# Retention and two feed-forward layers on one core: the lead-in in another order, with the first splits on VectorE

## The chip, the cores and the metric

The kernel runs on one core of a Trainium2 chip. The metric is the device time of one execution in microseconds (us); a kernel's figure is the median of several runs. A profile is one execution recorded by the hardware profiler; its span is a little shorter than the run's time. The engines are TensorE (PE; its weight loads are listed as PEld), VectorE (DVE), ScalarE (ACT), GpSimd (POOL) and SyncE (SP), which here issues all transfers.

## The reference

Retention with a decay per head (2 batches, 8 heads, 768 positions, head size 64), then two feed-forward layers on the 1536 x 512 result, all in float32:

```python
for t in range(S):
    state = gamma[None, :, None, None] * state + np.einsum('bhd,bhe->bhde', k[:, :, t], v[:, :, t])
    y[:, :, t] = scale * np.einsum('bhd,bhde->bhe', q[:, :, t], state)
...
x = np.ascontiguousarray(attn_out.transpose(0, 2, 1, 3)).reshape(B * S, H * D)
h = x @ w_in                                        # layer 1: 512 x 2048
g = np.maximum(h, 0.0) + np.log1p(np.exp(-np.abs(h)))
x = g @ w_out                                       # 2048 x 512
h = x @ w_in                                        # layer 2, other weights
g = h * (1.0 / (1.0 + np.exp(-h)))
out = g @ w_out
```

## The kernel before

**Retention in chunks.** A chunk is 128 positions of one batch. There are 12, numbered n = 0 to 11, and an even n and the next are the same positions of the two batches. For each chunk the kernel computes the scores (`att_scores`, L169, PE), multiplies them by the decay mask while it takes them out of PSUM (`att_mask`, L177, DVE), multiplies by V (`att_within`, L187), adds what the state of earlier chunks gives (`att_across`, L201, with `past`, the state copied by ACT at L159, and with queries scaled on GpSimd, `att_scale_q`, L128), and adds its own keys and values to the state (`att_state`, L149, with keys scaled on GpSimd, `att_scale_k`, L136). Chunks 0 and 1 have no across part. In names, `sc` are scores in PSUM, `scm` masked scores, `qp` and `kp` the scaled queries and keys, `py` a chunk's result in PSUM.

**Products in three parts.** The feed-forward products are made from a high and a low part of each operand: low times high, high times low, high times high. `att_split` makes the parts of a chunk's result: xhi is a rounded copy by ACT (L219), xlo the rest. With `spare=True` (chunks 0 and 1), ACT makes a second, unrounded copy (L222) and GpSimd subtracts (L223); otherwise DVE subtracts straight from PSUM (L225). Four chunks, all in one pair of tiles, are a block of 512 tokens.

**Weights** come as 64-bit floats, in units of 512 KB (128 x 512 values); unit u of the plan is converted by `w_exponent` (ACT, z, L272), then `convert`: `w_digits` (DVE, two operations, L279 and L280), `w_values` (DVE, four operations, L289 to L297, the last gives the low part wlo) and `w_split` (ACT, whi, L308, from the result `a` of L292). Three buffers hold raw units.

**The feed-forward steps.** `gemm1(i, half)` is 12 matmuls for half a tile h of hidden values: for i = 0 the halves are token columns 0 to 255 (chunks 0, 1) and 256 to 511 (chunks 2, 3), for others halves of the contraction. `act1` (ACT, L352 and L353) applies the function twice, rounded and not; `act2` (DVE, L359) subtracts. In the lead-in all h tiles share one bank of PSUM, so h1 can be written once `act1(0)` has read h0. `first(i)` is both halves and `act1`; `second(i)` is the second product.

**What sets the order.** The program is written in a fixed order, and each engine takes its instructions in the order in which the code emits them. All transfers are issued by SP in the order of the calls `att_load`, `qs_load`, `w_load` and of the single ones for `mask` and `cs`. `att_load(n, lo, hi)` loads parts lo to hi of chunk n: 0 and 1 are Q and K transposed (512 KB for the pair), 2 is V (256 KB), 3 is K (256 KB). The mask has 512 KB, `qs` 256 KB, `cs` 24 KB. The lead-in is L458 to L545; from L547 on, the later chunks alternate with feed-forward steps, and from L578 on there are feed-forward steps alone.

Of the kernel before, what the change touches and what calls it, by code (L numbers as in the profile page):

```python
# [75 lines left out]
def retention_ffn2_kernel(  # L76
# [133 lines left out]
    def att_split(n, spare=False):  # L210
        py = py_t.pop(n)
        blk, o = n // CPB, (n % CPB) * P
        if o == 0:
            x_t[0, blk] = (
                xpool.tile([P, NPAIR, BLK], F32R, tag="xhi", name=f"xhi{blk}"),
                xpool.tile([P, NPAIR, BLK], F32R, tag="xlo", name=f"xlo{blk}"),
            )
        hi, lo = (t[:, :, o : o + P] for t in x_t[0, blk])
        nc.scalar.activation(out=hi, in_=py, func=AF.Copy)  # L219
        if spare:  # L220
            full = epool.tile([P, NPAIR, P], F32, tag="t", name=f"y{n}")
            nc.scalar.activation(out=full, in_=py, func=AF.Copy)  # L222
            nc.gpsimd.tensor_tensor(out=lo, in0=full, in1=hi.bitcast(F32), op=ALU.subtract)  # L223
        else:
            nc.vector.tensor_tensor(out=lo, in0=py, in1=hi.bitcast(F32), op=ALU.subtract)  # L225
# [201 lines left out]
    def first(i):  # L427
        gemm1(i, 0)
        gemm1(i, 1)
        act1(i)  # L430
# [26 lines left out]
    with tc.manual_schedule():  # L457
# [5 lines left out]
        w_load(0)  # L463
        att_load(2, 0, 2)
        nc.sync.dma_start(out=cs, in_=cs_d)
        att_load(0, 3, 4)
        att_load(1, 3, 4)
        qs_load(1)
        att_load(3, 0, 2)
# [3 lines left out]
        att_load(4, 0, 2)  # L473
        att_load(2, 3, 4)
        att_load(3, 3, 4)
        nc.scalar.preload_act_table_set("softplus")
# [10 lines left out]
        att_split(0, spare=True)  # L487
        w_exponent(0)
        att_within(1)
        att_split(1, spare=True)  # L490
        convert(0)
        att_scores(2)
# [6 lines left out]
        qs_load(2)  # L499
        att_load(4, 2, 3)  # L500
        att_load(5, 2, 3)
        w_load(2)
        att_load(4, 3, 4)
        att_load(5, 3, 4)
        att_mask(2)
        att_scale_q(2)
        att_scale_q(3)
        att_scores(3)
        att_mask(3)
        att_within(2)  # L510
        att_across(2)
        w_exponent(1)
        w_digits(1)
        att_split(2)
        att_within(3)
        att_across(3)
        att_split(3)
        gemm1(0, 0)
        att_scale_k(2)
        att_scale_k(3)  # L520
        att_state(2)
        att_state(3)
        att_past()
# [4 lines left out]
        w_values(1)  # L528
        w_split(1)
        att_scale_q(4)  # L530
        att_scale_q(5)
        att_scores(4)
        att_scores(5)
        att_mask(4)
        att_mask(5)
        gemm1(0, 1)
        act1(0)
# [3 lines left out]
        att_scale_k(5)  # L541
        w_exponent(2)
        first(1)
        convert(2)
        act2(0)  # L545
# [98 lines left out]
```

## Time and profile before

| | before |
|---|---|
| time, median of 3 runs | 584.91 us (584.90 to 585.33) |
| profiled execution: time | 584.48 us |
| profiled execution: span | 582.3 us |
| PE busy in the span | 571.3 us (98%) |
| DVE, ACT, POOL busy | 372.4, 198.9, 46.4 us |
| the chain that ended last, by engine | PE 96%, DMA 1%, POOL 1% |
| first matmul of `first(1)` | 33.38 us |

The chain of work that ended last is followed back from the last instruction, at each step to what released it. Work that isn't on it costs nothing by itself. The granted clock (PEclk) is a share of 2.4 GHz.

### The profile page before, as it was taken

The numbers are of one execution on the slowest core, as the hardware profiler recorded it, in microseconds if no ns is written. First come the engines' busy times: TensorE is split into PE (matmuls) and PEld (weight loads), VectorE is DVE, ScalarE is ACT, GpSimd is POOL, SyncE is SP. The second block draws the span as 40 slices with busy tenths as digits, with TensorE's granted clock in tenths as the row PEclk, the third lists the DMA queues.
The fourth block names the chain that finished last, engine by engine and source line by source line (L and its number), as shares of the span: only waits on it lengthen the run. The fifth ranks groups of instructions, "written<-read, shape, count | busy, mean of one in ns | idle before, by whom it ended". The sixth has DMA issues, their size and how long they took to land.

```text
span 582.3 us, 7525 instructions
## 1 busy us (share of the span) xinstructions
PE 571.3 (98%) x3026; PEld 472.8 (81%) x3026; DVE 372.4 (64%) x611; ACT 198.9 (34%) x365; POOL 46.4 (8%) x38
## 2 busy tenths in 40 slices
PE   7899999999999999999999999999999999999997
PEld 4788888888888888888888888888888888888885
DVE  4889565755864866685769954575656854783332
ACT  2234153432432432342445542452333332342120
POOL 1816100000000000000213210000000000000000
PEclk9799999999999999999999999999999999999999
DMA  8987212311321222123113212122113212110111
GB/s 298 354 307 257 71 38 72 109 36 38 109 73 36 73 72 70 39 81 101 37 45 121 88 38 72 37 89 93 36 37 107 75 36 73 38 35 0 73 72 73
DMA packets 15731, 51.10 MB, mean 88 GB/s; under 512 B 1873, under 2 KB 1873, under 8 KB 15441
## 3 DMA queue, kind: packets, MB, share of 16 engines
q1 hardware_dynamic: 15696, 50.63, 25.2%
q8 instruction: 24, 0.39, 0.3%
q14 instruction: 11, 0.08, 0.1%
HBM read 47.47 MB, written 3.15 MB: 87 GB/s over the span
## 4 chain that ended last, share of the span: by engine, by line
PE 96%; DMA 1%; POOL 1%; ACT 0%; issue 0%; SPq 0%; DVE 0%; POOLq 0%
PE h L336 45%; PE acc L375 45%; PE py L187 2%; PE sc L169 2%; PE py L201 2%; DMA att<-in_att 1%; PE state L149 1%; POOL kp L136 0%; POOL xlo L223 0%; SPq L123 0%; DVE part L390 0%; ACT ghi L352 0%; ACT xhi L219 0%; ACT t L353 0%; ACT y L222 0%
## 5 line engine op out<-in xcount | busy, mean ns | idle before, releaser
L352 ACT ACTIVATE ghi<-h 128x512 fp32r<-128x512 f32 x96 | 57.4, 598 | 336.0 <-PE h L336 324.7
L359 DVE TENSOR_TENSOR glo<-t,ghi 128x512 fp32r<-128x512 f32 x96 | 66.5, 697 | 40.6 <-ACT t L353 40.6
L390 DVE TENSOR_TENSOR part<-acc,part 128x512 f32<-128x512 f32 x84 | 57.4, 692 | 50.0 <-PE acc L375 50.0
L336 PE MATMUL h<-xhi,wlo 128*128 128x512 f32 (+1 forms) x196 | 76.0, 388 | 1.2 <-ACT t L353 1.2
L289 DVE TENSOR_SCALAR z<-z 128x512 uint32<-128x512 uint32 x64 | 30.2, 472 | 71.1 <-ACT z L272 71.1
L336 PE MATMUL h<-xlo,whi 128*128 128x512 f32 (+1 forms) x196 | 75.4, 385 | 0.0
L336 PE MATMUL h<-xhi,whi 128*128 128x512 f32 (+1 forms) x196 | 75.4, 385 | 0.0
L375 PE MATMUL acc<-ghi,wlo 128*128 128x512 f32 x192 | 74.8, 390 | 0.0
L375 PE MATMUL acc<-ghi,whi 128*128 128x512 f32 x192 | 74.7, 389 | 0.0
L375 PE MATMUL acc<-glo,whi 128*128 128x512 f32 x192 | 74.7, 389 | 0.0
L336 PE MATMUL h<-yhi,wlo 128*128 128x512 f32 x192 | 74.7, 389 | 0.0
L336 PE MATMUL h<-ylo,whi 128*128 128x512 f32 x192 | 74.7, 389 | 0.0
L336 PE MATMUL h<-yhi,whi 128*128 128x512 f32 x192 | 74.7, 389 | 0.0
L375 PE MATMUL acc<-whi,glo 128*128 128x512 f32 x192 | 74.7, 389 | 0.0
L375 PE MATMUL acc<-wlo,ghi 128*128 128x512 f32 x192 | 74.7, 389 | 0.0
L375 PE MATMUL acc<-whi,ghi 128*128 128x512 f32 x192 | 74.7, 389 | 0.0
L353 ACT ACTIVATE t<-h 128x512 f32<-128x512 f32 x96 | 56.9, 593 | 0.0
L280 DVE SCALAR_TENSOR_TENSOR m<-raw,m 128x512 uint32<-128x512 uint32 x64 | 48.0, 749 | 2.2
L292 DVE SCALAR_TENSOR_TENSOR a<-raw,z 128x512 uint32<-128x512 uint32 x64 | 46.0, 719 | 2.2
L297 DVE SCALAR_TENSOR_TENSOR wlo<-m,z 128x512 fp32r<-128x512 int32 x64 | 46.0, 719 | 2.2
L336 PEld LDWEIGHTS h<-xhi,wlo 128*128 128x128 f32 x196 | 36.8, 188 | 9.1 <-ACT t L353 1.4
L308 ACT ACTIVATE whi<-a 128x512 fp32r<-128x512 f32 x64 | 40.5, 632 | 6.9 <-DVE a L292 6.9
(43 smaller groups left out, 697.1 us busy)
## 6 DMA issues: line engine op xcount, KB each, us to landing
raw<-in_wts SPq DMA_DIRECT2D x64, 512.0 KB, 3.3
att<-in_att SPq DMA_DIRECT2D x10, 512.0 KB, 6.6
att<-in_att SPq DMA_DIRECT2D x12, 256.0 KB, 7.4
out<-part SPq DMA_DIRECT2D x12, 256.0 KB, 2.0
att<-in_att SPq DMA_DIRECT2D x2, 1024.0 KB, 7.7
att<-in_att SPq DMA_DIRECT2D x2, 768.0 KB, 5.4
qs<-in_qs SPq DMA_DIRECT2D x5, 256.0 KB, 6.9
mask<-in_mask SPq DMA_DIRECT2D x1, 512.0 KB, 5.5
```

What stands on the lines that cost most here:

```text
L169: nc.tensor.matmul(pj[j][:, p, :], lhsT=a[r, 1, s], rhs=a[r, 0, s], start=True, stop=True)
L280: nc.vector.scalar_tensor_tensor(out=m, in0=raw[:, :, 1], scalar=23, in1=m, op0=ALU.logical_shift_left, op1=ALU.bitwise_or)
L289: nc.vector.tensor_scalar(out=z, in0=z, scalar1=3, scalar2=4, op0=ALU.logical_shift_left, op1=ALU.bitwise_or)
L292: nc.vector.scalar_tensor_tensor(out=a, in0=raw[:, :, 1], scalar=0x80000000, in1=z, op0=ALU.bitwise_and, op1=ALU.bitwise_or)
L297: nc.vector.scalar_tensor_tensor(out=lo, in0=m.bitcast(I32), scalar=2.0**-43, in1=z.bitcast(F32), op0=ALU.mult, op1=ALU.mult)
L308: nc.scalar.activation(out=hi, in_=a, func=AF.Copy)
L336: nc.tensor.matmul(ph[:, t], lhsT=w[:, s], rhs=x[:, kc, t], start=kc == o == j == 0, stop=kc == NPAIR - 1 and j == 2, skip_group_check=i == 0,
L352: nc.scalar.activation(out=ghi, in_=ph, func=f)
L353: nc.scalar.activation(out=t, in_=ph, func=f)
L359: nc.vector.tensor_tensor(out=glo, in0=t, in1=ghi.bitcast(F32), op=ALU.subtract)
L375: nc.tensor.matmul(acc_t[m], lhsT=lhsT, rhs=rhs, start=(first and j == 0), stop=(last and j == 2))
L390: nc.vector.tensor_tensor(out=part[:, m, :], in0=acc_t[m], in1=part[:, m, :], op=ALU.add)
```

## The change

In the queue of transfers, `cs`, the K parts of chunks 0 and 1, the Q and K of chunk 3 and the scale of the queries, which were behind the first weights, and the Q and K of chunk 2, which were right behind them, are moved ahead of them; the Q and K of chunk 4 are moved behind the K parts of chunks 2 and 3. Chunks 0 and 1 are split by DVE as the others are. The states of chunks 0 and 1 are computed ahead of scores 2; the scores and masks of chunks 2 and 3 stand ahead of the first conversion; both within products stand ahead of the across products; both halves of `gemm1(0)` stand together ahead of states 2 and 3; the second conversion stands behind the splits of chunks 2 and 3, with all its parts together, and `first(1)` ahead of the third one.

```diff
-    def att_split(n, spare=False):
+    def att_split(n):
...
         nc.scalar.activation(out=hi, in_=py, func=AF.Copy)
-        if spare:
-            full = epool.tile([P, NPAIR, P], F32, tag="t", name=f"y{n}")
-            nc.scalar.activation(out=full, in_=py, func=AF.Copy)
-            nc.gpsimd.tensor_tensor(out=lo, in0=full, in1=hi.bitcast(F32), op=ALU.subtract)
-        else:
-            nc.vector.tensor_tensor(out=lo, in0=py, in1=hi.bitcast(F32), op=ALU.subtract)
+        nc.vector.tensor_tensor(out=lo, in0=py, in1=hi.bitcast(F32), op=ALU.subtract)
...
@@ -460,19 +455,19 @@
         att_load(1, 2, 3)
-        w_load(0)
-        att_load(2, 0, 2)
         nc.sync.dma_start(out=cs, in_=cs_d)
         att_load(0, 3, 4)
         att_load(1, 3, 4)
+        att_load(2, 0, 2)
+        att_load(3, 0, 2)
         qs_load(1)
-        att_load(3, 0, 2)
+        w_load(0)
         att_load(2, 2, 3)
         att_load(3, 2, 3)
         w_load(1)
-        att_load(4, 0, 2)
         att_load(2, 3, 4)
         att_load(3, 3, 4)
+        att_load(4, 0, 2)
...
         att_within(0)
-        att_split(0, spare=True)
-        w_exponent(0)
+        att_split(0)
         att_within(1)
-        att_split(1, spare=True)
-        convert(0)
-        att_scores(2)
+        att_split(1)
         att_scale_k(0)
         att_scale_k(1)
         att_state(0)
         att_state(1)
         att_past()
         att_load(5, 0, 2)
-        qs_load(2)
         att_load(4, 2, 3)
         att_load(5, 2, 3)
+        qs_load(2)
         w_load(2)
         att_load(4, 3, 4)
         att_load(5, 3, 4)
+        att_scores(2)
         att_mask(2)
+        att_scores(3)
+        att_mask(3)
         att_scale_q(2)
         att_scale_q(3)
-        att_scores(3)
-        att_mask(3)
+        w_exponent(0)
+        convert(0)
         att_within(2)
+        att_within(3)
+        w_exponent(1)
         att_across(2)
-        w_exponent(1)
-        w_digits(1)
         att_split(2)
-        att_within(3)
         att_across(3)
         att_split(3)
         gemm1(0, 0)
+        gemm1(0, 1)
         att_scale_k(2)
         att_scale_k(3)
         att_state(2)
         att_state(3)
+        convert(1)
+        act1(0)
         att_past()
...
         w_load(3)
-        w_values(1)
-        w_split(1)
...
         att_scores(4)
+        att_mask(4)
         att_scores(5)
-        att_mask(4)
         att_mask(5)
-        gemm1(0, 1)
-        act1(0)
...
+        first(1)
+        act2(0)
         w_exponent(2)
-        first(1)
         convert(2)
-        act2(0)
         act2(1)
```

In the rows below numbers of chunks are left out of the names and the last number is a tile's own. On SP, behind the Q and K of chunk 1 and the V of chunk 0, the queue of before goes on as follows (att_92 is chunk 0, att_95 chunk 1, att_101 chunk 2, att_108 chunk 3, raw_0_99 and raw_0_112 the first two weight units):

```order
L123 DMA att_95<-in_att 128x512
L264 DMA raw_0_99<-in_wts 128x1024
L123 DMA att_101<-in_att 128x1024
L465 DMA cs<-in_cs 128x48
L123 DMA att_92<-in_att 128x512
L123 DMA att_95<-in_att 128x512
L115 DMA qs_106<-in_qs 128x512
L123 DMA att_108<-in_att 128x1024
L123 DMA att_101<-in_att 128x512
L123 DMA att_108<-in_att 128x512
L264 DMA raw_0_112<-in_wts 128x1024
```

In the changed kernel the same place reads (att_102 is chunk 2, att_104 chunk 3, raw_0_108 and raw_0_112 the weight units):

```order
L123 DMA att_95<-in_att 128x512
L458 DMA cs<-in_cs 128x48
L123 DMA att_92<-in_att 128x512
L123 DMA att_95<-in_att 128x512
L123 DMA att_102<-in_att 128x1024
L123 DMA att_104<-in_att 128x1024
L115 DMA qs_106<-in_qs 128x512
L259 DMA raw_0_108<-in_wts 128x1024
L123 DMA att_102<-in_att 128x512
L123 DMA att_104<-in_att 128x512
L259 DMA raw_0_112<-in_wts 128x1024
```

The first weights went from the second place of these rows to the eighth, behind `cs`, the K parts of chunks 0 and 1, both Q and K pairs of chunks 2 and 3 and the scale of the queries.

On DVE, from the masks of chunk 1 to those of chunk 3, before (scm_0_148 and scm_1_150 are chunk 1, scm_0_234 and scm_1_236 chunk 2, scm_0_252 and scm_1_254 chunk 3; m, z, a and wlo are the conversion of the first unit):

```order
L177 TENSOR_TENSOR scm_0_148<-sc_0_138,mask 128x512
L177 TENSOR_TENSOR scm_1_150<-sc_1_139,mask 128x512
L279 TENSOR_SCALAR m_0_183<-raw_0_99 128x512
L280 SCALAR_TENSOR_TENSOR m_0_183<-raw_0_99,m_0_183 128x512
L289 TENSOR_SCALAR z_0_167<-z_0_167 128x512
L292 SCALAR_TENSOR_TENSOR a_0_168<-raw_0_99,z_0_167 128x512
L295 TENSOR_SCALAR z_0_167<-a_0_168 128x512
L297 SCALAR_TENSOR_TENSOR wlo_0_189<-m_0_183,z_0_167 128x512
L177 TENSOR_TENSOR scm_0_234<-sc_0_193,mask 128x512
L177 TENSOR_TENSOR scm_1_236<-sc_1_194,mask 128x512
L177 TENSOR_TENSOR scm_0_252<-sc_0_242,mask 128x512
L177 TENSOR_TENSOR scm_1_254<-sc_1_243,mask 128x512
```

Now, from behind the masks of chunk 1 (scm_0_217 and scm_1_219 are chunk 2, scm_0_231 and scm_1_233 chunk 3):

```order
L220 TENSOR_TENSOR xlo_162<-py_152,xhi_161 128x4x128
L220 TENSOR_TENSOR xlo_162<-py_165,xhi_161 128x4x128
L177 TENSOR_TENSOR scm_0_217<-sc_0_207,mask 128x512
L177 TENSOR_TENSOR scm_1_219<-sc_1_208,mask 128x512
L177 TENSOR_TENSOR scm_0_231<-sc_0_221,mask 128x512
L177 TENSOR_TENSOR scm_1_233<-sc_1_222,mask 128x512
L274 TENSOR_SCALAR m_0_242<-raw_0_108 128x512
L275 SCALAR_TENSOR_TENSOR m_0_242<-raw_0_108,m_0_242 128x512
L284 TENSOR_SCALAR z_0_239<-z_0_239 128x512
L287 SCALAR_TENSOR_TENSOR a_0_240<-raw_0_108,z_0_239 128x512
L290 TENSOR_SCALAR z_0_239<-a_0_240 128x512
L292 SCALAR_TENSOR_TENSOR wlo_0_248<-m_0_242,z_0_239 128x512
```

Two subtractions and the four masks of chunks 2 and 3 moved ahead of the six operations of the conversion.

On ACT, from the split of chunk 0 on, before (xhi_161 with py_152, py_170, py_256 and py_281 are chunks 0 to 3; y is the unrounded copy; whi_0_191 belongs to the first unit, z_0_273 and whi_0_349 to the second):

```order
L219 ACTIVATE xhi_161<-py_152 128x4x128
L222 ACTIVATE y_164<-py_152 128x512
L272 ACTIVATE z_0_167<-raw_0_99 128x512
L219 ACTIVATE xhi_161<-py_170 128x4x128
L222 ACTIVATE y_180<-py_170 128x512
L308 ACTIVATE whi_0_191<-a_0_168 128x512
L159 ACTIVATE past<-state 128x512
L272 ACTIVATE z_0_273<-raw_0_112 128x512
L219 ACTIVATE xhi_161<-py_256 128x4x128
L219 ACTIVATE xhi_161<-py_281 128x4x128
```

Now (py_152, py_165, py_252 and py_261 are chunks 0 to 3; whi_0_250 belongs to the first unit, z_0_270 and whi_0_348 to the second, ghi and t are `act1(0)`):

```order
L219 ACTIVATE xhi_161<-py_152 128x4x128
L219 ACTIVATE xhi_161<-py_165 128x4x128
L159 ACTIVATE past<-state 128x512
L267 ACTIVATE z_0_239<-raw_0_108 128x512
L303 ACTIVATE whi_0_250<-a_0_240 128x512
L267 ACTIVATE z_0_270<-raw_0_112 128x512
L219 ACTIVATE xhi_161<-py_252 128x4x128
L219 ACTIVATE xhi_161<-py_261 128x4x128
L303 ACTIVATE whi_0_348<-a_0_271 128x512
L347 ACTIVATE ghi_350<-h_293 128x512
L348 ACTIVATE t_351<-h_293 128x512
```

The unrounded copies are gone, the first unit's exponent and whi moved behind `past`, ahead of the split of chunk 2, and the second unit's whi stands ahead of `act1(0)` as before.

## Rows read from the trace of the kernel before

**Rows 1.** Stages: us, length, busy time of each engine, PEclk, DMA share, GB/s.
```profile
12.90:25.83 12.93, 10.54 (x129) 8.98 (x129) 11.35 (x12) 2.83 (x5) 11.14 (x9) 0.74 1.03 392
25.83:33.38 7.55, 6.38 (x91) 5.85 (x89) 6.70 (x10) 2.85 (x6) 3.67 (x4) 1.00 0.70 222
33.38:45.00 11.62, 11.62 (x148) 10.02 (x149) 9.36 (x16) 4.46 (x8) 2.71 (x3) 1.00 0.86 321
```

**Rows 2.** The chain that ended last, in order of time: start, us, what.
```profile
2.11 7.35 DMA att<-in_att
...
11.89 1.27 POOL xlo L223
...
14.80 2.68 POOL kp L136 x2
...
18.64 2.01 PE sc L169 x16
...
25.90 1.62 PE h L336 x12
27.52 1.08 PE state L149 x32
28.60 1.99 PE sc L169 x32
...
32.24 0.60 ACT ghi L352
...
33.38 3.02 PE h L336 x12
...
38.29 1.89 PE py L201 x32
```

**Rows 3.** Timeline of PE: start, us, instruction, count, idle time before and releaser.
```profile
12.90 1.16 PE L169 MATMUL sc<-att 64*128 64x128 f32 x16 [1.31 <-DMA att<-in_att]
...
16.07 1.07 PE L149 MATMUL state<-att,kp 128*64 128x64 f32 x16 [2.01 <-POOL kp L136]
```

**Rows 4.** Stages of one microsecond, columns as in group 1.
```profile
15.00:16.00 1.00, 0.00 (x0) 0.00 (x0) 0.96 (x2) 0.00 (x0) 1.00 (x2) 1.00 1.01 379
16.00:17.00 1.00, 0.93 (x16) 0.88 (x16) 0.96 (x2) 0.40 (x1) 1.00 (x2) 0.59 1.08 418
```

**Rows 5.** Timeline of SP: issue of att3's and of att4's Q and K.
```profile
9.48 0.33 SPq L123 DMA_DIRECT2D att<-in_att  x1
...
13.15 0.43 SPq L123 DMA_DIRECT2D att<-in_att  x1
```

**Rows 6.** The same two transfers in the DMA view: size, us from issue to landing.
```profile
att<-in_att SPq DMA_DIRECT2D x1, 512.0 KB, 6.7
...
att<-in_att SPq DMA_DIRECT2D x1, 512.0 KB, 6.9
```

**Rows 7.** Timeline of DVE, columns as in group 3.
```profile
9.16 1.29 DVE L177 TENSOR_TENSOR scm<-sc,mask 128x512 f32<-128x512 f32 x2 [0.24 <-PE sc L169]
...
15.15 1.41 DVE L292 SCALAR_TENSOR_TENSOR a<-raw,z 128x512 uint32<-128x512 uint32 x1
...
17.78 1.64 DVE L297 SCALAR_TENSOR_TENSOR wlo<-m,z 128x512 fp32r<-128x512 int32 x1
...
26.57 0.69 DVE L225 TENSOR_TENSOR xlo<-py,xhi 128x512 fp32r<-128x512 f32 x1 [1.35 <-ACT xhi L219]
...
33.37 0.41 DVE L279 TENSOR_SCALAR m<-raw 128x512 uint32<-128x512 uint32 x1
...
36.06 0.69 DVE L297 SCALAR_TENSOR_TENSOR wlo<-m,z 128x512 fp32r<-128x512 int32 x1
```

**Rows 8.** Timeline of POOL, columns as in group 3.
```profile
22.04 2.61 POOL L136 TENSOR_TENSOR kp<-att,cs 128x512 f32<-128x512 f32 x2 [1.48 <-DMA att<-in_att]
24.71 2.63 POOL L128 TENSOR_TENSOR qp<-att,qs 128x512 f32<-128x512 f32 x2
```

## The prediction

> **What bounds the kernel now.** I read the stages first, then the chain that ended last, then the timelines of VectorE (DVE), GpSimd (POOL) and the DMA queue (SP) in the first 40 us. From 33.38 us on TensorE (PE) is never idle in the stage shown, 11.62 us busy of 11.62; before that it is busy 10.54 of 12.93 us and 6.38 of 7.55 us [rows 1]. So the kernel is bound by PE, and the lead-in is where time can still go. The work on PE ahead of the second h product, `first(1)`, is the same set of instructions in both kernels: the three warm-up products, scores, within and across of chunks 0 to 3, the states, both halves of `gemm1(0)`, scores 4 and 5. The question is thus one number: when does `first(1)` start. Before it is 33.38 us, and the piece ahead of it is ScalarE's (ACT) `act1(0)`, 1.14 us from 32.24 [rows 2]: product h1 waits for the bank of h0.
>
> Going back along the chain [rows 2]: loads until 9.46 (2.11 + 7.35), GpSimd's first subtraction at 11.89, its two kp at 14.80 (2.68 us), then PE without a break from 17.5. GpSimd is thus late because of the two splits. PE's states had stood waiting for kp for 2.01 us up to 16.07 [rows 3], and here a second cost begins: the granted clock is 1.00 in 15 to 16 us and 0.59 in 16 to 17 [rows 4], so it fell near 16.2. The stage of 12.93 us has a mean of 0.74 [rows 1]; at the two levels 1.2 and 2.4 GHz (0.5 and 1.0) that is 0.52 of the stage, 6.7 us, at the lower one. Sixteen score pieces took 2.01 us there and 32 took 1.99 us later [rows 2]: half speed, so some 3 us were lost.
>
> **The loads.** SP's queue keeps eight transfers in flight: that of att3 was issued at 9.48, just when the V part of chunk 0, eight before it in the queue, landed at 9.46 [rows 2, 5]. Landings follow the order of issue: 9.46 is the landing of KB 1792 of the queue, att3 (KB 4376) landed at 9.48 + 6.7 = 16.2, att4 (KB 5912) at 13.15 + 6.9 = 20.05 [rows 5, 6]. That is 0.67 and 0.64 us per 256 KB; I take 0.66. In the new order: V of chunk 1 at 10.1, cs (24 KB) 10.2, the K parts of chunks 0 and 1 at 10.85 and 11.5, att2 12.8, att3 14.15, queries' scale qs1 14.8, first weights raw0 16.1, V parts 16.8 and 17.4, raw1 18.8, K parts 19.4 and 20.1, att4 21.4. Transfers after 20 us can be later: GpSimd got the K part of chunk 2 at 22.04, 1.3 us behind that pace [rows 8]. I keep 0 and 1.3 us as bounds for all after 19 us.
>
> **The splits.** Two ACT copies go (0.5 us of ACT each, off the path), two GpSimd subtractions go (11.89 to 14.80), two DVE subtractions come. A split on DVE read 0.69 us, and read the same while GpSimd worked (26.57, beside qp from 24.71 to 27.34) [rows 7, 8]. DVE has nothing else from 10.45 (masks 1, 9.16 + 1.29) to 15.2 (masks 2), since raw0 now lands at 16.1, so they cost nothing. If they were slow (1.4 us each) they would still end before scores 2: that is the cover. GpSimd now starts kp0 when K and cs are there: 10.9 + 2.68 = 13.6 instead of 17.47.
>
> **To the first weights.** State 1 ends 0.55 us after 13.6 (32 pieces take 1.08 at full clock), 14.15; scores 2 and 3 follow at 1.0 each, 16.15 [rows 2]. Masks take 1.29 us a chunk [rows 7]: 15.2 to 16.5 to 17.8. Within 2 waits for V at 16.8, within 3 ends at 18.75, both across at 20.65 (1.89 for the two) [rows 2]; qp (2.63) is ready by 17.45.
>
> Now the new order turns against itself: the first conversion stands behind masks 2 and 3 on DVE, and can't start before 17.8. Alone, a conversion's six operations take 3.4 us (33.37 to 36.75) [rows 7]. That gives 21.2. Beside GpSimd its operations with both inputs in SBUF stretch: three took 4.27 us from 15.15 to 19.42, 1.42 each [rows 7], while kp and qp ran [rows 2]. K of chunk 2 lands at 19.4 and kp2, kp3 then run; the four operations begun by then end at 20.0, the last two at 20.0 + 2 x 1.42 = 22.85. Bounds: 21.2 if kp comes 1.3 us later, 23.6 if three are hit. I take 22.85. On ACT the second exponent and xhi2, xhi3 are queued behind whi0, which waits for that conversion's fourth operation (20.0); they end near 22.3, still ahead of DVE, which does xlo2 and xlo3 only after the conversion.
>
> **From there to `first(1)`.** PE: `gemm1(0,0)` at 22.85 for 1.62, `gemm1(0,1)`, now directly behind it, for as much to 26.1 (its xlo3 is there at 24.2); states 1.08 and scores 4, 5 1.99 [rows 2]: 29.15. DVE: second conversion from 24.2, three operations alone 1.5, three beside qp4, qp5 and kp4 4.27: 30.0. (qs2 lands between 24.7 and 25.9, so that collision comes either way.) ACT: whi1 after the fourth operation, 27.1 + 0.65, then `act1(0)` 1.14: h0 is read by 28.9. The latest is DVE: `first(1)` at **30.0**, 3.4 us earlier than 33.38. What was the end of the path, `act1(0)`, goes; the weights' low part is late next.
>
> After that I see nothing given back. Masks 4 and 5 (2.5 us from 30.0) end 0.5 us before PE asks for them at 33.0; scores 6 want att6 and att7 at 36.8 (33.0 and two times 1.9), and 4352 KB behind the K part at 20.1 they land by 31.3, 32.6 with the slip. The loads of u=3 and u=4 swap places on SP; u=3, 1536 KB later and behind the fourth operation of the second conversion, lands by 36.5, and its conversion stands behind masks 6 and 7, past 39.
>
> **The clock.** The sum has PE at full clock. PE would stand still for 0.7 us before each state and before within 2, and for 2.2 us from 20.65 to 22.85. The pause of 2.01 us in the trace preceded a fall [rows 3, 4]; but of the 4.5 us up to its end (1.31 + 1.16 + 2.01) PE had worked only 1.16, and here it works without a break of note for 3.8 us before. I take the full clock, and keep the fall as a rival.
>
> The Trainium skill, page "TensorE: Matmul & The Clock Gate", section "Why this matters for your kernels", asks only for no pauses over about 3 us between bursts of products. By that rule no pause here is long enough and the time stays at the forecast; the row of 2.01 us speaks against the rule, and by the row alone the second rival below would hold.
>
> **The sum.** The profiled execution took 584.48 us (span 582.3) where the median is 584.91, 0.43 above. 3.4 off gives 581.1 for such an execution and **581.5** for the median. 0.2%, 1.17 us, is about what a measurement of this kernel can tell from no change.
>
> **Rivals.**
> *No collisions.* If GpSimd is late both times, the first conversion ends at 21.2, xlo3 at 23.0, the second conversion at 26.4, PE's scores 5 at 27.6, so `first(1)` at 27.6: 5.8 us off, 579.1. For it: the 1.3 us slip of loads after 20 us. Against: three operations must miss GpSimd twice, and qs2 lands in the middle of the second.
> *The clock falls* in the pause before `gemm1(0,0)`. With a stretch like that of before (6.7 us) from 22 on, PE does in 5.85 us what takes 2.9: scores 5 end at 32.1, past DVE's 30.0, and 1.3 us are gained: 583.6. With a short stretch 30.0 to 31 holds, because PE had 0.85 us to spare.
> *Slower: the clock stays low.* If the early pauses (11.6 to 13.6) make it fall, PE's chain grows by half the low stretch, from 29.15. It passes 33.38 when more than 8.5 us are at the lower level, against 6.7 before. Twice that of before, 13.4 us, gives 35.85: 2.5 us slower, 587.4. For it: the work up to 20 us is small products with waits on masks between. Against: the pause of 1.31 us ahead of 12.90 left the clock at 1.00 [rows 3, 4].
> *It doesn't do what it says.* If the loads land so late that GpSimd's kp0 isn't before 14, all moves back by 3 us: within 0.2%. The pace of the landings speaks against it.
>
> **Chances.** Forecast 0.45, no collisions 0.14, clock falls 0.28, slower 0.10, no effect 0.03. The fall holds 0.13 faster, 0.13 same and 0.02 slower: **faster 0.72, same 0.16, slower 0.12**. The range goes from no collisions, 579.0, to a fall that leaves little, 584.6; outside are the slower case, the worst falls and a few in a hundred below.
>
> **What would show it.** Right: kp0 near 11 us, masks 2 and 3 ending near 18, the first wlo at 21 to 24, `first(1)` near 30 with DVE's wlo as what it waited for, and the same distance to the end behind it. Wrong: a PEclk of 0.5 for over 8 us before 33, a wait of scores 6 for att6, or `first(1)` released by `act1(0)` past 32.

## The result

| | before | after |
|---|---|---|
| time, median of 6 runs each | 585.12 us (584.26 to 585.90) | 578.32 us (577.85 to 579.88) |
| ratio | | 0.989 (95% interval 0.9874 to 0.9905) |
| profiled execution: time, span | 584.48, 582.3 us | 577.85, 575.9 us |
| start of `first(1)` | 33.38 us | 26.86 us |
| from there to the end of the span | 548.9 us | 549.0 us |

The change takes off 6.8 us where 3.4 were forecast; 578.3 lies below the range, which began at 579.0. In the profiled execution all of the gain stands ahead of `first(1)`, which starts 6.5 us earlier. Two later series of the same kernel, each with the kernel before beside it, gave 580.12 us (10 executions; ratio 0.9938, 0.9913 to 0.9963), which would lie inside the range, and 578.42 (6 executions; 0.9919, 0.9889 to 0.9950). Of all 22 executions, 577.85 to 583.99 us, 15 are below 580 and 7 at 580.9 or more. This scatter is part of the result, and an experiment below is about it.

The stages of after (us, length, busy time of PE, PEld, DVE, ACT and POOL, PEclk, DMA share, GB/s; [rows 1] are those of before):

```profile
12.90:25.83 12.93, 11.75 (x186) 10.71 (x184) 10.45 (x18) 4.64 (x9) 4.62 (x5) 1.00 1.04 398
25.83:33.38 7.55, 7.55 (x96) 6.46 (x92) 7.25 (x11) 3.10 (x6) 4.92 (x4) 1.00 1.03 407
33.38:45.00 11.62, 11.62 (x170) 9.99 (x168) 11.48 (x15) 5.15 (x10) 5.75 (x4) 1.00 1.01 402
```

PE is now busy for 11.75 of 12.93 us in the stage in which it was for 10.54, and PEclk is 1.00 where it was 0.74. The stretch at 1.2 GHz is gone. In the third row DVE is busy for 11.48 of 11.62 us: PE never waits there, but DVE has next to no idle time.

The chain of after that ended last, in order of time (start, us, what), answers to [rows 2]:

```profile
3.94 6.51 DMA att<-in_att
...
10.60 2.06 POOL kp L136 x2
...
12.70 0.69 PE state L149 x16
13.38 1.14 PE sc L169 x16
...
20.88 0.52 DVE xlo L220
...
21.49 0.69 DVE xlo L220
...
22.22 1.57 PE h L331 x11
23.79 1.08 PE state L149 x32
24.87 1.99 PE sc L169 x32
26.86 2.94 PE h L331 x12
```

Scores 5 end at 26.86 and `first(1)` follows without a gap: it waits neither for DVE, as was forecast, nor for ACT, as before. Why DVE isn't late shows in its timeline (start, us, instruction, count, idle before):

```profile
16.91 0.42 DVE L274 TENSOR_SCALAR m<-raw 128x512 uint32<-128x512 uint32 x1
...
19.61 0.69 DVE L292 SCALAR_TENSOR_TENSOR wlo<-m,z 128x512 fp32r<-128x512 int32 x1
20.88 1.29 DVE L220 TENSOR_TENSOR xlo<-py,xhi 128x512 fp32r<-128x512 f32 x2 [0.58 <-ACT xhi L219]
22.09 0.74 DVE L274 TENSOR_SCALAR m<-raw 128x512 uint32<-128x512 uint32 x1
...
25.11 0.69 DVE L292 SCALAR_TENSOR_TENSOR wlo<-m,z 128x512 fp32r<-128x512 int32 x1
```

and in that of GpSimd:

```profile
14.48 2.50 POOL L128 TENSOR_TENSOR qp<-att,qs 128x512 f32<-128x512 f32 x2 [1.84 <-DMA qs<-in_qs]
20.50 2.05 POOL L136 TENSOR_TENSOR kp<-att,cs 128x512 f32<-128x512 f32 x2 [3.50 <-PE py L201]
25.77 2.53 POOL L128 TENSOR_TENSOR qp<-att,qs 128x512 f32<-128x512 f32 x2 [3.22 <-DMA qs<-in_qs]
```

The first conversion runs from 16.91 to 20.30, 3.4 us: alone. kp2 starts 0.2 us after its end. The second runs from 22.09 to 25.80 (its first operation, 0.74 us instead of 0.42, meets the end of kp3), and qp4 starts just as it ends. Neither of the two collisions of the forecast took place, and by small margins. The wait ahead of kp2 is put down to PE, whose across products end then too, but it was for the K part of chunk 2, issued at 11.13 and landed 9.2 us later, at 20.33 (timeline of SP, then the DMA view):

```profile
11.13 0.33 SPq L123 DMA_DIRECT2D att<-in_att  x1
...
att<-in_att SPq DMA_DIRECT2D x1, 256.0 KB, 9.2
```

In a run below, in which K lands earlier, kp2 starts at 19.25, while the across products run on until 20.8.

The diff holds one more move, which the list ahead of it leaves out: `qs_load(2)` went behind the V parts of chunks 4 and 5, 512 KB later in the queue. qs2 is what qp4 waits for until 25.77. At the pace of the prediction (0.66 us per 256 KB) it would have landed some 1.3 us earlier in its old place, an estimate, and qp4 would have met the second conversion. No run tests this move alone.

### The profile page after: what moved, and what is told of

It reads as the page before. It is cut to its first block, busy times and chain, and to the rows that moved or that the text cites. A ratio compares the mean times of both kernels' runs of the same rounds, so it can differ in the third digit from the quotient of the medians.

```text
span 575.9 us, 7532 instructions
## 1 busy us (share of the span) xinstructions
PE 568.8 (99%) x3026; PEld 470.2 (82%) x3026; DVE 370.1 (64%) x613; ACT 197.9 (34%) x363; POOL 43.4 (8%) x36
## 3 DMA queue, kind: packets, MB, share of 16 engines
q1 hardware_dynamic: 15696, 50.63, 25.2%
## 4 chain that ended last, share of the span: by engine, by line
PE 96%; DMA 1%; DVE 1%; SPq 1%; POOL 0%; ACT 0%; issue 0%; DVEq 0%; POOLq 0%
PE acc L370 45%; PE h L331 45%; PE sc L169 2%; PE py L201 1%; PE py L187 1%; DMA att<-in_att 1%; PE state L149 1%; POOL kp L136 0%; SPq L123 0%; DVE scm L177 0%; DVE xlo L220 0%; DVE a L287 0%; DVE m L275 0%; DVE part L385 0%; ACT whi L303 0%
## 5 line engine op out<-in xcount | busy, mean ns | idle before, releaser
L354 DVE TENSOR_TENSOR glo<-t,ghi 128x512 fp32r<-128x512 f32 x96 | 68.1, 714 | 40.4 <-ACT t L348 40.4
L284 DVE TENSOR_SCALAR z<-z 128x512 uint32<-128x512 uint32 x64 | 28.2, 441 | 71.2 <-ACT z L267 71.2
L275 DVE SCALAR_TENSOR_TENSOR m<-raw,m 128x512 uint32<-128x512 uint32 x64 | 45.4, 710 | 2.2
L267 ACT ACTIVATE z<-raw 128x512 f32<-128x512 f32 x64 | 42.7, 668 | 1.6 <-DMA raw<-in_wts 1.6
```

What stands on the lines that cost most here:

```text
L267: nc.scalar.activation(out=z, in_=raw_t[u][:, :, 1].bitcast(F32), func=AF.Copy, scale=2.0**-112)
L275: nc.vector.scalar_tensor_tensor(out=m, in0=raw[:, :, 1], scalar=23, in1=m, op0=ALU.logical_shift_left, op1=ALU.bitwise_or)
L284: nc.vector.tensor_scalar(out=z, in0=z, scalar1=3, scalar2=4, op0=ALU.logical_shift_left, op1=ALU.bitwise_or)
L354: nc.vector.tensor_tensor(out=glo, in0=t, in1=ghi.bitcast(F32), op=ALU.subtract)
```

## The experiments

Where a time of `first(1)` is given, it is that of the run's profile; "rest" is the span behind it, 548.9 us before and 549.0 after.

### Do the parts have shares of the gain?

**Splits alone** (kernel before):

```diff
-        att_split(0, spare=True)
+        att_split(0, spare=False)
...
-        att_split(1, spare=True)
+        att_split(1, spare=False)
```

> The kernel before with one edit: chunks 0 and 1 are split by VectorE. Theory A (GpSimd's start and its collisions with the conversions set the lead-in): kp0 starts at 13.5 us (K and cs landed) instead of 14.8, but the first conversion still runs beside kp and qp and ends near 19.4, so first(1) starts between 31.5 and 33.4: 0 to 2 us off, 583 to 585. Theory B (the gain is the stretch at 1.2 GHz that is gone): TensorE's pause before the states shrinks from 2.0 to 0.8 us, the clock stays at 1.00 and some 3 us or more are gained: 582 or less.

Measured 585.68 us, ratio 1.0023 (1.0010 to 1.0036); `first(1)` at 34.51. GpSimd is free earlier, but its kp and qp still run beside the first conversion, which stands ahead of masks 2 on DVE and ends at 20.0; PE waits 2.9 us for those masks and its clock falls there instead (0.61 and 0.54 in the two stretches of 2 us from 22 us). Theory A had the mechanism but not the loss. Theory B's condition, a clock that stays at 1.00, did not come about: the pause before the states became short (0.8 us), and the clock fell elsewhere. The run doesn't decide on what the clock is worth; a run below with added products does.

**Loads alone** (kernel before, the transfers' calls as in the changed kernel):

```diff
-        w_load(0)
-        att_load(2, 0, 2)
...
+        att_load(2, 0, 2)
+        att_load(3, 0, 2)
         qs_load(1)
-        att_load(3, 0, 2)
+        w_load(0)
...
-        att_load(4, 0, 2)
...
+        att_load(4, 0, 2)
```

> The kernel before with one edit: the transfers in the changed order. Theory A: the first weights land at 15.6 us instead of 11.4, their conversion stands ahead of masks 2 and runs beside GpSimd's kp and qp, ends near 21.5, and all moves back by about 2 us: 586 to 588. A rival, that earlier keys and queries by themselves are the gain: 583 or less.

Measured 588.26 us, 1.0071 (1.0043 to 1.0099); `first(1)` at 36.78. The size is a little above what was expected, and the reason was mostly another one: of the first conversion only the last two operations were slow (1.38 and 1.41 us). In the old order of ACT the first exponent stands between the splits of chunks 0 and 1; it now waits for raw0, and with it the second unrounded copy, GpSimd's second subtraction and both kp, for which PE waits 6.6 us. GpSimd's timeline in this run:

```profile
11.76 1.26 POOL L223 TENSOR_TENSOR xlo<-y,xhi 128x512 fp32r<-128x512 f32 x1 [11.32 <-ACT y L222]
17.77 1.62 POOL L223 TENSOR_TENSOR xlo<-y,xhi 128x512 fp32r<-128x512 f32 x1 [4.75 <-DMA raw<-in_wts]
19.34 2.67 POOL L136 TENSOR_TENSOR kp<-att,cs 128x512 f32<-128x512 f32 x2
```

**Order alone** (kernel before, the calls behind the warm-up as in the changed kernel, with `spare=True` and the old transfers):

```diff
-        convert(0)
-        att_scores(2)
...
+        att_mask(3)
...
+        w_exponent(0)
+        convert(0)
```

> The kernel before with one edit: the program's order of the changed kernel, with the old order of the transfers and the old splits. Theory A: kp0 waits for the splits on GpSimd and starts at 14.8 us, masks end past 20, both conversions collide: no gain, 584 to 587. A rival, that the order is the gain and loads and splits add little: 581 or less.

Measured 587.53 us, 1.0061 (1.0040 to 1.0082), a little above theory A's bounds; `first(1)` at 35.95. kp0 starts at 14.11, and the masks of chunk 3 end at 22.4. Only the first conversion collides (three of its operations take 1.26 to 1.64 us, it ends at 28.2); the second runs alone.

**All but the loads** (changed kernel, transfers as before):

```diff
+        w_load(0)
+        att_load(2, 0, 2)
         nc.sync.dma_start(out=cs, in_=cs_d)
...
```

> The changed kernel with one edit undone: the transfers in the old order. Theory A: kp0 waits for K at 13.5 us (10.6 in the changed kernel), masks 2 and 3 end near 19.8, the conversions meet kp2, kp3 (from 22) and qp4, qp5, and first(1) starts at 30 to 31.5: 3 to 5 us more than the changed kernel, 581 to 583. Theory B: the time follows the clock; if the granted clock stays at 1.00 it is within 2 us of the changed kernel, below 580.5.

Measured 585.59 us, 1.0030 (1.0010 to 1.0050): nothing is left of the gain, a larger loss than theory A expected. kp waits for K until 13.93, PE waits 3.1 us for kp and its clock falls (0.77 and 0.50 in the two stretches of 2 us from 14 us), so theory B, which speaks of a clock that stays up, isn't tested. Both conversions have operations of 1.15 to 1.41 us. `first(1)` starts at 33.55, and 4 us more are lost behind it (rest 553.2 in a profiled execution that was one of the longest): PE waits 2.5 us for a late xlo at 54 us, and its clock falls again (0.51 in 56 to 58 us).

**All but the splits** (changed kernel, `spare=True` for chunks 0 and 1):

```diff
-        att_split(0)
+        att_split(0, spare=True)
```

> The changed kernel with one edit undone: chunks 0 and 1 are split by a second ScalarE copy and GpSimd. Theory A: GpSimd is busy to 14.0 us with the splits, kp0 starts there, masks 2 and 3 end near 20.3, both conversions collide with kp2, kp3 and qp4, qp5, first(1) near 31.5: 582 to 583.5. Theory B: TensorE's pause from 11.5 to 15 us makes the clock fall; 1.5 to 3 us more on top, 584 to 586.

Measured 585.12 us, 1.0004 (0.9993 to 1.0016); `first(1)` at 33.31. PE waited 3.7 us for kp, and the clock fell (0.66 and 0.50 in the two stretches from 16 us), as theory B had it. Theory A's two collisions were one: the first conversion ran alone, only late (21.88 to 25.27 us; in the changed kernel it starts at 16.91, and 3.7 of the 5.0 us between them are the later kp); the second met qp4 and kp4 and took 6.1 us (27.03 to 33.16) instead of 3.7.

So no part has a share of its own: splits +0.2%, loads +0.7%, order +0.6%, and the whole without the loads or without the splits gains nothing. (The whole without the new order was not run.) In all five kp0 is late (it starts at 13.4 to 19.3 us instead of 10.60), and at least one of the two conversions runs beside kp or qp again. In all five the clock fell as well, to 0.50 to 0.54 for a stretch of 2 us or more. These runs thus can't tell the price of the collisions from that of the clock; the next three do so in part.

### What did the stretch at 1.2 GHz cost?

**Two more warm-up products** in the kernel before, in the pause ahead of the states:

```diff
         att_scores(2)
+        for _ in range(2):
+            nc.tensor.matmul(warm, lhsT=zero[:, :P], rhs=zero, start=True, stop=True)
```

> The kernel before with two more warm-up products on TensorE behind scores 2, which fill 1.7 of the 2.01 us of the pause before the states. Theory B (the stretch at 1.2 GHz costs what it looks like): the clock stays at 1.00 and first(1) starts 2 to 3.3 us earlier, 582 to 583. Theory A: the clock stays at 1.00, but VectorE's late masks and conversions hold TensorE instead, and 0.5 to 2 us are gained: 583 to 584.6.

Measured 583.24 us, 0.9977 (0.9965 to 0.9988). The clock stayed at 1.00 throughout and `first(1)` started at 32.22, 1.2 us earlier (in a profiled execution that lost 1.1 us again to a late xlo at 53 us). The kernel before took 584.69 us in this series, so the fall of the clock costs the old order some 1.3 us, not the 3 us that the stretch seems to lose: DVE's masks and conversions come next. Theory A holds. Keeping the clock up is by itself worth a fifth of the 6.8 us. What a fall would cost in the new order, where DVE is no longer late, this run doesn't show.

### Do collisions cost what the prediction said?

**Three unused products on GpSimd beside the first conversion** (changed kernel):

```diff
         att_scale_q(3)
+        for _ in range(3):
+            nc.gpsimd.tensor_tensor(out=zero, in0=a_t[0][:, 3, :], in1=a_t[1][:, 3, :], op=ALU.mult)
```

> The changed kernel with three products added on GpSimd that nothing uses, from 17.0 to about 20.7 us, beside the first conversion. Theory A (as the prediction had it: a conversion's operations take 1.4 us each beside GpSimd, and a late first conversion makes the second one meet qp4 and qp5): the first wlo ends at 22.5 to 23.5 instead of 20.3, the second at 28.5 to 29.5 instead of 25.8, first(1) starts at 28.5 to 29.5: 2 to 2.7 us more than the changed kernel, near 580.7. A rival, that the price of a collision was too high: under 0.7 us more.

Measured 585.79 us, 1.0027 (1.0010 to 1.0044): 7.5 more than the first series of the changed kernel (which was not run beside this one), three times what was expected. `first(1)` started at 33.88. Five of the six operations were hit (they ran beside GpSimd and took longer), 1.15 to 1.64 us each, as kp2 and kp3 followed the three products, and the first wlo ended at 25.2. PE had stood still for 4.4 us, and its clock fell to 0.50: 24 products of `gemm1(0)` took 5.49 us where they take 3.1. Later PE waits another 2.7 us for an xlo. The run isn't clean: the products hold the buffer of chunk 0, into which chunk 5 is loaded, so qs2 came late and the second conversion ran alone (26.30 to 29.68).

**The same behind kp3, beside the second conversion** (reading chunks 2 and 3):

```diff
         att_scale_k(3)
+        for _ in range(3):
+            nc.gpsimd.tensor_tensor(out=zero, in0=a_t[2][:, 3, :], in1=a_t[3][:, 3, :], op=ALU.mult)
```

> The changed kernel with the same three products on GpSimd behind kp3, from 22.5 to 26.3 us, beside the second conversion alone; qp4 moves to 26.3. Theory A: the second wlo ends at 28 to 29, TensorE waits for it from 26.9 on, first(1) at 28 to 29: 1.2 to 2.2 us more than the changed kernel. A rival, that the conversions have slack there: no difference.

Measured 583.42 us, 0.9989 (0.9977 to 1.0001): 5 more than the first series of the changed kernel. DVE in this run:

```profile
22.95 1.66 DVE L275 SCALAR_TENSOR_TENSOR m<-raw,m 128x512 uint32<-128x512 uint32 x1
24.54 1.49 DVE L284 TENSOR_SCALAR z<-z 128x512 uint32<-128x512 uint32 x1
26.05 1.64 DVE L287 SCALAR_TENSOR_TENSOR a<-raw,z 128x512 uint32<-128x512 uint32 x1
27.73 1.37 DVE L290 TENSOR_SCALAR z<-a 128x512 uint32<-128x512 uint32 x1
29.14 1.63 DVE L292 SCALAR_TENSOR_TENSOR wlo<-m,z 128x512 fp32r<-128x512 int32 x1
```

GpSimd's added products are one piece beside them:

```profile
22.59 4.55 POOL L517 TENSOR_TENSOR zero<-att,att 128x512 f32<-128x512 f32 x3
```

These operations, all of whose inputs are in SBUF, take 1.4 to 1.7 us beside GpSimd and 0.4 to 0.7 alone, and GpSimd's products take 1.52 each where qp, of the same size, takes 1.25: both pay. The price in the prediction, 1.42, was about right: the ten operations that were hit in these two runs took 1.15 to 1.66 us, 1.51 in the mean. What theory A left out came behind it: PE stood still for 3.6 us, and `first(1)`, from 30.91, took 4.35 us instead of 2.94 at a PEclk of 0.62 and 0.53.

**K of chunks 2 and 3 earlier** (changed kernel), about when the forecast had it:

```diff
-        w_load(1)
         att_load(2, 3, 4)
         att_load(3, 3, 4)
+        w_load(1)
```

> The changed kernel with the K parts of chunks 2 and 3 queued ahead of raw1 instead of behind it. Theory A (the prediction's collisions happen when GpSimd gets its keys before the first conversion is done): K lands near 18.5 instead of 20.3, kp2 and kp3 run beside the first conversion, the first wlo ends at 22 to 23.5, the second conversion meets qp4 from 25.8, first(1) starts at 29 to 31: 3 to 4 us more than the changed kernel, the time that was predicted. A rival, that other work than GpSimd's keys decides: within 1 us.

Measured 582.35 us, 0.9970 (0.9957 to 0.9983). kp2 starts at 19.25, as the prediction had it (19.4), and DVE does what it said of the first conversion (timelines of GpSimd and of DVE):

```profile
19.25 2.40 POOL L136 TENSOR_TENSOR kp<-att,cs 128x512 f32<-128x512 f32 x2 [1.79 <-DMA att<-in_att]
...
18.88 0.69 DVE L287 SCALAR_TENSOR_TENSOR a<-raw,z 128x512 uint32<-128x512 uint32 x1
19.61 1.15 DVE L290 TENSOR_SCALAR z<-a 128x512 uint32<-128x512 uint32 x1
20.79 1.41 DVE L292 SCALAR_TENSOR_TENSOR wlo<-m,z 128x512 fp32r<-128x512 int32 x1
...
26.02 1.64 DVE L292 SCALAR_TENSOR_TENSOR wlo<-m,z 128x512 fp32r<-128x512 int32 x1
```

The first wlo ends at 22.2 (forecast 22.85). Of the second conversion, which starts 0.9 us before the forecast's, only the last operation is hit; it ends at 27.7, and `first(1)` starts at 28.46 behind PE's own chain, 1.6 us later than in the changed kernel and ahead of the 29 to 31 expected. The rest is lost where I had seen nothing: at 48.5 us PE waits for the xlo of chunks 6 and 7 (timeline of PE), and then the clock falls (stages):

```profile
50.36 0.50 PE L331 MATMUL h<-xlo,whi 128*128 128x512 f32 x1 [1.85 <-DVE xlo L220]
```

```profile
48.00:50.00 2.00, 0.51 (x5) 0.19 (x1) 2.00 (x3) 1.15 (x2) 2.00 (x3) 1.00 0.61 177
50.00:52.00 2.00, 1.64 (x7) 1.33 (x7) 2.00 (x4) 0.00 (x0) 1.01 (x2) 0.92 0.58 230
52.00:54.00 2.00, 2.00 (x6) 1.32 (x4) 1.97 (x5) 0.00 (x0) 0.00 (x0) 0.50 0.06 17
54.00:56.00 2.00, 2.00 (x25) 1.74 (x26) 1.90 (x5) 1.60 (x3) 0.00 (x0) 0.73 0.06 25
```

The rest of this run is 552.5 us (581.0 - 28.46), 3.5 more than in the changed kernel: 1.85 for the wait, the others for the clock. So the time came out near the expected one, but more than half of what this execution loses is of another kind than theory A's.

**K of chunks 2 and 3 later**:

```diff
-        att_load(2, 3, 4)
-        att_load(3, 3, 4)
         att_load(4, 0, 2)
+        att_load(2, 3, 4)
+        att_load(3, 3, 4)
```

> The changed kernel with the same K parts queued behind the Q and K of chunk 4. Theory A: kp2 and kp3 run from 21.7 to 23.9 us, beside the first operations of the second conversion, and that one then meets qp4 too: first(1) at 28 to 30.5, 1.5 to 4 us more than the changed kernel. A rival, that an early GpSimd is what costs: no difference.

Ratio 0.9949 (0.9926 to 0.9972): seven executions took 578.9 to 582.9 us, 581.1 in the median; an eighth took 1864.8 us, with no cause on record, and isn't counted. kp2 ran from 21.73, beside the first operations of the second conversion, qp4 met the last one, and `first(1)` started at 27.90. PE waits 1.9 us at 48 us here too, with the clock at 1.00 behind it. That is the direction that theory A expected and less than its size. Beside the changed kernel in the same series (0.9938, 0.9913 to 0.9963) the early place is slower at the edge of the intervals, and the late one can't be told apart from it by time; by the start of `first(1)` both are later, 28.46 and 27.90 against 27.23 in that series' profile of the changed kernel.

### A shorter chain

**kp0 and kp1 on DVE**, ahead of the splits (changed kernel):

```diff
-    def att_scale_k(n):
+    def att_scale_k(n, eng=None):
...
-        nc.gpsimd.tensor_tensor(
+        (eng or nc.gpsimd).tensor_tensor(
...
         att_within(0)
-        att_split(0)
         att_within(1)
-        att_split(1)
-        att_scale_k(0)
-        att_scale_k(1)
+        att_scale_k(0, nc.vector)
+        att_scale_k(1, nc.vector)
+        att_split(0)
+        att_split(1)
```

> The changed kernel with kp0 and kp1 made by VectorE, ahead of the two splits. Theory A (the chain K part, kp, states, scores 2, masks, conversions sets the time): two operations of 0.7 us in place of 2.04, states end at 12.5 instead of 13.4, all of the chain moves up by 0.8 us, first(1) at 26.0: 577.5. A rival, that loads (raw0 15.6, V 16.4, qs2 25.7) end last: no difference.

Measured 580.40 us, 0.9941 (0.9920 to 0.9962): not better. The states did end at 13.1, but in the profiled execution within 2 waited for its V part until 17.02, and within 3 started at 18.96, 2 us after its masks were done (its V part, issued at 10.60, landed 8.2 us later, at 18.8), so that all behind it was late; `first(1)` at 28.08, and again 1.9 us of wait at 48 us with a fall of the clock behind it.

### What makes the scatter?

**The changed kernel again**, two series:

> The changed kernel itself, as a yardstick for the runs beside it. If its gain rests on kp2 and qp4 falling between the conversions (in its trace kp2 starts 0.2 us behind the first wlo, qp4 at the end of the second), executions in which a load lands otherwise must be slower by one to several us: a spread of 2 us or more, 578 to 581. If it rests on the order of the program alone, all executions lie within 0.3%.

> The changed kernel once more, as the yardstick on this chip: executions from 578 to 584 as before, median 578.5 to 580.5.

The first gave 578.05 to 583.99 us, four of ten at 582 or more; the second 578.32 to 583.06, two of six. Their mean granted clock is 0.996 to 0.999 in those from 580.9 up and 0.999 or 1.000 in the others. Both profiles were of short executions (578.26 and 578.32 us) and show what the first one shows; no long execution has a trace.

**GpSimd held until a conversion is done** (a tiny product that reads wlo of unit u, ahead of kp2 with u = 0 and ahead of qp4 with u = 1):

```diff
+    def hold(u):
+        w, s, _ = plan[u]
+        lo = w_t[w, s][1].bitcast(F32)
+        nc.gpsimd.tensor_tensor(out=zero[:, :16], in0=lo[:, :16], in1=lo[:, :16], op=ALU.mult)
...
+        hold(0)
         att_scale_k(2)
...
+        hold(1)
         att_scale_q(4)
```

> The changed kernel with two tiny products on GpSimd (128 x 16) that read the low part of the first and of the second weights, ahead of kp2 and of qp4, so that GpSimd cannot start beside the first two conversions. Theory A (executions differ by 6 us because in some of them kp2 or qp4 comes before a conversion is done): the executions of 581 to 584 are gone, all lie at 578 to 580, median 578.5. A rival, that late V parts or the fourth conversion (which meets qp6 and kp6 from 39 us on) make the slow executions: the spread stays.

> The kernel that holds GpSimd until the first and the second weights are converted, once more for its spread. Of 22 executions of the changed kernel 7 took 580.9 us or more. Theory A (GpSimd beside the first two conversions makes them): none here, all at 578 to 580. A rival: about one in three above 580.5.

**qs3 ahead of chunk 8**:

```diff
-        att_load(8)
         qs_load(3)
+        att_load(8)
```

> The changed kernel with the scale qs3 queued ahead of chunk 8 instead of behind it. qp6 no longer waits for it until 39.3 us but runs from 34 on beside masks, and the fourth conversion (38 to 45 us in the changed kernel, three operations stretched) runs alone. If TensorE's wait of 1.9 us at 50 us for a late xlo, seen in the two runs with moved K parts, is what slow executions have: the spread shrinks and the median falls to 578.5. Theory A (the first two conversions): the spread stays, the slow executions lose at most 1.9 us.

> The kernel with qs3 ahead of chunk 8, once more for its spread. Theory A: nothing in it keeps GpSimd out of the first two conversions, so executions of 580.5 us or more occur, about one in three. A rival (the fourth conversion makes them): none.

**Both**:

> Both edits of the two runs before it together. Theory A with the second wait: all executions at 578 to 579, median 578.2, which is the best of the changed kernel made the rule. A rival, that what is left of the spread is in the landing of the loads up to 17 us: the median stays between 579 and 581.

| | executions | us | medians | ratio to before |
|---|---|---|---|---|
| changed kernel | 22 | 577.85 to 583.99 | 578.32, 580.12, 578.42 | 0.9890, 0.9938, 0.9919 |
| GpSimd held | 9 | 578.12 to 580.86 | 579.53, 579.30 | 0.9903, 0.9900 |
| qs3 ahead | 8 | 577.84 to 579.26 | 578.10, 578.15 | 0.9887, 0.9882 |
| both | 4 | 578.02 to 578.62 | 578.43 | 0.9888 |

Theory A isn't borne out for the scatter: in the kernel with qs3 moved nothing keeps GpSimd out of the first two conversions, and none of its eight executions is long (at 7 in 22 that would happen once in some 20 tries). The counts don't settle it, though: the held kernel has none above 580.9 in nine either (one is at 580.86), and the long executions of the changed kernel come unevenly, none in six, five in ten and two in six. The traces say more, and they point to the fourth conversion. In the changed kernel GpSimd's qp6 waits for qs3 until 39.26 us:

```profile
39.26 3.16 POOL L128 TENSOR_TENSOR qp<-att,qs 128x512 f32<-128x512 f32 x2 [8.50 <-DMA qs<-in_qs]
42.37 2.68 POOL L136 TENSOR_TENSOR kp<-att,cs 128x512 f32<-128x512 f32 x2
45.01 2.99 POOL L128 TENSOR_TENSOR qp<-att,qs 128x512 f32<-128x512 f32 x2
```

and DVE, in its fourth conversion from 38.12 on, has xlo7, the low part of chunk 7, at 46.79 (45.52 + 1.27):

```profile
38.12 0.41 DVE L274 TENSOR_SCALAR m<-raw 128x512 uint32<-128x512 uint32 x1
...
39.63 1.65 DVE L287 SCALAR_TENSOR_TENSOR a<-raw,z 128x512 uint32<-128x512 uint32 x1
41.31 1.38 DVE L290 TENSOR_SCALAR z<-a 128x512 uint32<-128x512 uint32 x1
42.73 1.41 DVE L292 SCALAR_TENSOR_TENSOR wlo<-m,z 128x512 fp32r<-128x512 int32 x1
44.07 1.53 DVE L354 TENSOR_TENSOR glo<-t,ghi 128x512 fp32r<-128x512 f32 x1
45.52 1.27 DVE L220 TENSOR_TENSOR xlo<-py,xhi 128x512 fp32r<-128x512 f32 x2
```

PE asks for it at 46.90: 0.1 us of slack. In the run with early K the same conversion starts 1.5 us later, two operations more are hit, and PE waits 1.85 us and loses its clock, 3.5 us in all: about the distance between the short and the long executions. With qs3 ahead (it lands near 37, not by 34 as expected), qp6 starts at 37.09 and GpSimd's four pieces are over at 42.45, so a conversion that starts later is hit less, not more.

Two executions of the held kernel show the step by itself. In both `first(1)` starts at 27.20 and the fourth conversion near 38.75; qp6 starts at 39.37 in one (579.63 us, the first two rows) and at 39.80 in the other (578.69 us, the last two), and that decides whether one more operation is hit:

```profile
39.37 3.05 POOL L128 TENSOR_TENSOR qp<-att,qs 128x512 f32<-128x512 f32 x2 [7.54 <-DMA qs<-in_qs]
39.80 1.50 DVE L284 TENSOR_SCALAR z<-z 128x512 uint32<-128x512 uint32 x1
...
39.80 3.24 POOL L128 TENSOR_TENSOR qp<-att,qs 128x512 f32<-128x512 f32 x2 [7.96 <-DMA qs<-in_qs]
39.81 0.42 DVE L284 TENSOR_SCALAR z<-z 128x512 uint32<-128x512 uint32 x1
```

In the first PE waits 1.2 us for xlo7, and the span is 577.6 us; in the second it doesn't wait, and the span is 576.6. Two runs with a late `first(1)` say the same: with K later and qs3 in its old place it starts at 27.90 and the rest is 551.0 us, with both edits, and so qs3 ahead, it starts at 27.76 and the rest is 548.8 us, without a wait. So for kernels one small edit away the step is shown. That it makes the long executions of the changed kernel itself is argued, not shown, since none was traced. In both profiles of the version with qs3 ahead alone xlo7 has no slack either (PE waits some 0.2 us for it); with both edits it has. The version with qs3 ahead is the best one found: 578.1 us twice, without long executions so far.

## Why the prediction was wrong

| step | forecast | measured |
|---|---|---|
| kp0 starts, kp1 ends | 10.9, 13.6 | 10.60, 12.64 |
| state 1 ends | 14.15 | 13.38 |
| masks 3 end, first conversion starts | 17.8 | 16.9 |
| kp2 starts | 19.4 | 20.50 |
| first wlo | 22.85 | 20.30 |
| xlo3 | 24.2 | 22.17 |
| second wlo | 30.0 | 25.80 |
| scores 5 end | 29.15 | 26.86 |
| `first(1)` | 30.0 | 26.86 |

**Right**: the question (only the start of `first(1)` counts, and what follows is 549 us in both), the loads within 0.5 us up to 17 us, splits that cost nothing (DVE's two took 0.69 us each, with kp running), the chain through kp, states, scores and masks, the second half of `gemm1(0)` behind the first. The clock stayed up: the pause of 2.2 us for which a fall was feared did not come about, since the conversion was done.

**Wrong, the terms of the two conversions.** On DVE the forecast ended at 30.0 and the trace at 25.8. Of these 4.2 us, 0.9 come before the first conversion: the K part of chunk 0 is there 0.3 us earlier, and kp takes 1.02 us beside DVE's splits, not the 1.34 of a row in which DVE's conversion ran beside it [rows 2]. 1.7 are the first conversion (3.4 us instead of 5.05) and 2.2 the second (3.6 from the end of xlo3 instead of 5.8); xlo3, held by ACT's queue behind whi0, takes 0.5 back. PE's own chain, at 26.86, then became the end, which leaves 3.1 us. The step that failed is "K of chunk 2 lands at 19.4 and kp2, kp3 then run": K landed at 20.33, 0.9 behind the pace, and the conversion had begun 0.9 before its time. The first lay inside the bounds that the text gave (0 to 1.3 us); the second did not, since the conversion "can't start before 17.8" and started at 16.91. Together they crossed the edge between hit and not hit: done at 20.30, K there at 20.33. The run with early K shows the price of the first collision to be right: with kp2 at 19.25 the first wlo is at 22.2. That its time, 582.35 us, is near the forecast is luck: `first(1)` starts at 28.46 there, not at 30.0, and 3.5 us are lost behind it, where the prediction had nothing.

**Wrong, the chances.** "Three operations must miss GpSimd twice" treated the two misses as two pieces of luck. They hang together: once the first conversion misses kp2, the second starts early and is done about when qs2 lands (25.80 and 25.77; the bounds for qs2 were right). "That collision comes either way" went by a second conversion that ends at 26.4 even in the rival without collisions, behind the bounds for qs2 (24.7 to 25.9); the 0.9 us before the first conversion undid it. And where the first one is hit, in the run with early K, only one operation of the second is. The rival "no collisions" deserved more than 0.14; it gave 27.6 and 579.1 us, and with K and kp 0.9 us earlier that is what happened.

**Right as a case, wrong as a whole**: "after that I see nothing given back" holds for the traced executions of the changed kernel, all of them short ones. (Its 4352 KB are 3840 up to the Q and K of chunk 7; nothing hangs on it.) But DVE has 0.1 us of slack at 47 us, which the sum did not look at, and the three runs that start `first(1)` 1 to 2 us later, with qs3 in its old place, lose 2 to 4 us more there. The rivals in which the clock falls were not wrong in kind: with the conversion hit by added products it fell in the very pause named.

## What to carry to other kernels

When two engines slow each other down, their collisions are not independent costs: work the forecast out once with the first one happening and once without, and give the chances to whole chains. Where a start and an end that decide this lie within a microsecond of each other, both outcomes belong in the range. An engine that is busy for 99% of a stage without being waited for is the next one to look at: here moving what it meets there (qs3) gave 578.1 us, and shortening the chain ahead of it 580.4.

## What was not expected of the hardware

- GpSimd pays too: kp took 1.34 us each beside DVE's conversion [rows 2] and 1.02 beside its splits, an unused product 1.52 against 1.25 for qp.
- The clock fell after a pause of 1.85 us in dense work (the run with early K: 0.50 in 52 to 54 us, 2.4 GHz again by 56), and did not after one of 1.9 us at the same place in the run with late K. The Trainium skill, page "TensorE: Matmul & The Clock Gate", section "Why this matters for your kernels", asks only for no gaps over some 3 us; the first of these rows goes against that, and the fall cost about as much as the pause.
- The fall of the clock in the kernel before looks like 3 us and is worth 1.3: filling the pause gave 583.24 us against 584.69.
